# The front of an attention-plus-GLU kernel: value weights in two loads, a shorter inverse root, and another order of transpositions and products

## The chip, the cores and the metric

The kernel runs on one core of one Trainium2 chip. Its metric is the device time of one execution in microseconds; lower is better. Three runs of the kernel before gave 728.47, 729.49 and 730.18 us, so the median is 729.49 us.

## The reference

`x` is one sequence of 2048 tokens with 448 features. The output is `x` plus an attention branch plus a gated feed-forward branch, both fed by the same layer norm without scale and bias:

```
xn = (x - mean(x)) / sqrt(var(x) + 1e-5)
q, k, v = xn @ wq, xn @ wk, xn @ wv      # 16 heads of 28, four segments of 512 tokens
per segment: o = g * memory(q) + (1 - g) * softmax(q k^T / sqrt(28) + mask) v
             memory is then updated with phi(k)^T v and sum of phi(k)
h = sigmoid(xn @ w_gate) * (xn @ w_up)   # 448 -> 1792
out = x + o @ wo + h @ w_down
```

All values are float32. What matters here is the very beginning: the layer norm of the first segment, its transposition, and the products with `wv` and then with `wk` and `wq`.

## The kernel before, in words

**Numbers in two parts.** TensorE works on float32 operands in a rounded form ("high"). For exactness each operand is kept as a high part and the rest that rounding cut off ("low"), and a product is a sum over pairs high x high, high x low, low x high. 448 features are three chunks of 128 and one of 64. The lower half of chunk 3 of the activations holds the low part of its upper half, so a full product over 448 features takes eleven matrix instructions. The list `TERMS` (line 48) gives their order: for each chunk the three pairs, then the last two for chunk 3.

**Tiles.** A segment (a block `b`, four of them) is four tiles of 128 tokens. `acc[b]` holds the loaded `x`; `xs[b]` holds the normalised and transposed activations, high parts at chunk indices 0 to 3, low parts at 4 to 6 and in the lower half of chunk 3; `wv` and `wqk[c]` hold the split weights, high at 0 to 3, low at 4 to 7.

**What one tile of block 0 goes through.** VectorE takes mean and variance (`statistics`, lines 252 to 254). ScalarE takes the square root (`root`, 259). VectorE makes the reciprocal and refines it with one Newton step (`rstd`, 265 to 269), then normalises (`normalise`, 274) and copies 64 columns once more behind the row (275). TensorE transposes four pieces of 128x128 into one PSUM bank `pt` (96). ScalarE copies the bank to the high part of `xs` (98), VectorE subtracts to get the low part (99 for three chunks, 100 for the lower half of chunk 3). TensorE then makes the tile's values with eleven products into the bank `pv` (`values`, 284), and ScalarE moves them to `vst` (286).

**Weights.** `wv` arrives in four quarters, one for each chunk, in turns with the four tiles of `x` (349 and 350). Each quarter is rounded on ScalarE (365) and the rest subtracted on GpSimd (366). The weights for keys and queries arrive as seven chunks and are split the same way (370 and 371).

**What sets the order.** Within the front the queues of TensorE, ScalarE and VectorE hold the instructions in the order in which the program text issues them (`manual_schedule`, line 236), and each engine works through them in that order. So the text of lines 374 to 399, and the loop behind it, is the order table. It begins with `WARM` = 12 products of the identity with itself into a bank that nobody reads (375 and 376). After the fourth tile's values come seven groups of eleven products for keys and queries (`keys_queries`, 295, bank `pp`), during which VectorE and ScalarE also prepare block 1. Everything after that (feed-forward, attention, output) is one long list in which TensorE is nearly always busy.

Of the kernel before, what the change touches and what calls it, by code (L numbers as in the profile page):

```python
# [46 lines left out]

TERMS = [t for c in range(3) for t in ((c, c), (c, 4 + c), (4 + c, c))] + [(3, 3), (3, 7)]
# [4 lines left out]
WARM = 12  # L53
# [3 lines left out]
def kernel(  # L57
# [30 lines left out]
    def transpose_split(pt, src, dst, t):  # L88

        tok = slice(t * P, (t + 1) * P)  # L90
        for c in range(4):
            part = slice(c * P, (c + 1) * P)
            if src.dtype == F32R:
                T.transpose(pt[:, part].bitcast(F32R), src[:, part], ident_r)
            else:
                T.transpose(pt[:, part], src[:, part], ident)
        p3 = pt.rearrange("p (c n) -> p c n", c=4)
        A.activation(dst[:, 0:4, tok], p3, AF.Copy)  # L98
        V.tensor_sub(dst[:, 4:7, tok], p3[:, 0:3], dst[:, 0:3, tok].bitcast(F32))
        V.tensor_sub(dst[64:, 3, tok], p3[64:, 3], dst[64:, 3, tok].bitcast(F32))  # L100

# [134 lines left out]
    with tc.tile_pool(name="front", bufs=2) as sb, tc.manual_schedule(engines=FRONT):  # L236
# [9 lines left out]
        def statistics(b, t0, steps):  # L246
# [3 lines left out]
            ve = sb.tile([P, steps], F32, name=f"ve{steps}")  # L250
# [3 lines left out]
            V.tensor_scalar_add(ve, mv[:, :, 1], EPS)  # L254
            return mv, ve

        def root(ve):
            y = sb.tile([P, ve.shape[1]], F32, name=f"y{ve.shape[1]}")
            A.activation(y, ve, AF.Sqrt)
            return y  # L260

        def rstd(mv, ve, y):
            steps = ve.shape[1]
            tm = sb.tile([P, steps], F32, name=f"tm{steps}")
            V.reciprocal(y, y)
            V.tensor_mul(tm, y, y)
            V.tensor_mul(tm, tm, ve)
            V.tensor_scalar(tm, tm, -0.5, 1.5, op0=ALU.mult, op1=ALU.add)
            V.tensor_mul(y, y, tm)
            return [(mv[:, t, 0:1], y[:, t:t + 1]) for t in range(steps)]  # L270

        def normalise(b, t, mean, y):
            xn = sb.tile([P, 512], F32, name="xn")
            V.tensor_scalar(xn[:, :D], acc[b][:, t, :], mean, y, op0=ALU.subtract, op1=ALU.mult)
            (V if b == 0 else G).tensor_copy(xn[:, D:], xn[:, 384:D])
# [5 lines left out]
        def values(b, t):  # L281
            pv = bank("pv", "p")
            for n, (a, w) in enumerate(TERMS):
                T.matmul(pv[:, :D], xs[b][:, a, t * P:(t + 1) * P], wv[:, w, :],  # L284
                         start=n == 0, stop=n == len(TERMS) - 1)
            A.activation(vst[:, t, :, :DH], pv[:, :D].rearrange("p (h d) -> p h d", d=DH), AF.Copy)
# [59 lines left out]
        raw = [raw[t // 2][:, t % 2, :D] for t in range(4)]  # L346
        wv3 = w_v.rearrange("p (c n) -> p c n", c=4)
# [29 lines left out]
        mv, ve = statistics(0, 0, 1)  # L377
        y = root(ve)
        split_v(0)
        x0 = normalise(0, 0, *rstd(mv, ve, y)[0])  # L380
        split_v(1)
        split_v(2)
        mv, ve = statistics(0, 1, 1)
        y = root(ve)
        turn(0, 0, x0)
        split_v(3)
        x1 = normalise(0, 1, *rstd(mv, ve, y)[0])
        mv, ve = statistics(0, 2, 2)
        values(0, 0)
        turn(0, 1, x1)  # L390
        y = root(ve)
        st = rstd(mv, ve, y)
        split_qk(0)
        x2 = normalise(0, 2, *st[0])
        x3 = normalise(0, 3, *st[1])
        values(0, 1)
        turn(0, 2, x2)
        turn(0, 3, x3)
        split_qk(1)
        G.memset(heads, 1.0)  # L400
# [7 lines left out]
        for b in range(NB):  # L408
# [5 lines left out]
            for t in range(2 if b == 0 else 0, NT):  # L414
# [7 lines left out]
                if t == (3 if b == 0 else 0):  # L422
                    mv, ve = statistics(b + 1, 0, NT)
                if t == (3 if b == 0 else 0):
                    st = mv, ve, root(ve)
# [302 lines left out]
```

## Time and profile before

| what | value |
|---|---|
| median of three runs (lowest, highest) | 729.49 us (728.47, 730.18) |
| the profiled execution's own time | 728.81 us |
| span in the profile of that execution | 727.1 us |
| TensorE busy with matrix instructions | 708.5 us, 97% of the span |
| VectorE, ScalarE, GpSimd busy | 77%, 47%, 20% |
| first product for keys and queries starts | 26.04 us |
| first value product of block 1 starts | 51.25 us |

Times in the profile count from the start of the span, in microseconds. PE is TensorE, DVE is VectorE, ACT is ScalarE, POOL is GpSimd, SP issues the transfers. In a row of the timeline the first number is the start and the second the length; the name left of the arrow is written, the names right of it are read, xN is how many instructions the row joins, and the bracket gives the idle time ahead of it with what ended it. In a row of the table by windows each engine has its busy time and its count; then come the granted clock of TensorE (1.00 is full), the share of the transfer engines and the rate.

### The profile page before, as it was taken

To read this page: it belongs to the slowest core of one execution; us is meant where nothing else is said; L and a number is where in the kernel's file an instruction comes from. 1 tells how busy PE (TensorE), PEld (TensorE's weight loads), DVE (VectorE), ACT (ScalarE), POOL (GpSimd) and SP (SyncE) were. 2 spreads that over 40 slices of the span, in tenths; PEclk is the share of its full clock that TensorE was granted. 3 is DMA by queue.
4 is the path that set the end of the run, shared out by engine and by line. 5 is a ranking of instruction groups with operands and counts; after the bars stand their busy time and mean duration, and the time that the engine had idled before them with its cause. 6 is when DMAs were issued, how large, how long until landed. Compare 5 with 4: busy or idle time off the path is not lost.

```text
span 727.1 us, 10861 instructions
## 1 busy us (share of the span) xinstructions
PE 708.5 (97%) x3788; PEld 587.2 (81%) x3788; DVE 560.9 (77%) x1030; ACT 338.2 (47%) x552; POOL 147.9 (20%) x349
## 2 busy tenths in 40 slices
PE   7999999999999999999999999999999999998898
PEld 6888888887887877878878777787787877876697
DVE  5676776455599888898888898898788898888653
ACT  3635444231355554565545555455454555444320
POOL 4310000000131212222223223242222332322100
PEclk7999999999999999999999999999999999999999
DMA  9443546675343223322333225232422233223242
GB/s 311 185 174 133 218 178 236 227 252 134 98 106 86 74 66 94 107 78 67 109 103 88 59 83 133 71 88 79 127 66 73 64 92 85 82 74 110 84 159 89
DMA packets 58278, 86.24 MB, mean 119 GB/s; under 512 B 20080, under 2 KB 36976, under 8 KB 57712
## 3 DMA queue, kind: packets, MB, share of 16 engines
q1 hardware_dynamic: 56944, 81.88, 36.2%
q0 software_dynamic: 1280, 3.67, 1.4%
q8 instruction: 30, 0.49, 0.3%
q14 instruction: 24, 0.20, 0.1%
HBM read 53.81 MB, written 31.72 MB: 118 GB/s over the span
## 4 chain that ended last, share of the span: by engine, by line
PE 62%; DVE 18%; issue 8%; POOL 6%; ACT 3%; DMA 3%; SPq 0%; POOLq 0%; ACTq 0%; DVEq 0%
PE pgu L209 22%; PE pd L154 10%; PE pp L295 8%; PE pv L284 6%; PE po L668 5%; DVE mx L521 4%; DVE w L557 4%; PE st L506 3%; PE pa L583 3%; POOL w L518 2%; DVE acc L157 2%; DVE mb L549 2%; PE n L341 1%; PE pmm L323 1%; POOL on L595 1%
## 5 line engine op out<-in xcount | busy, mean ns | idle before, releaser
L209 PE MATMUL pgu<-xs,wgu 128*128 128x512 f32 x1232 | 321.7, 398 | 0.0
L209 PEld LDWEIGHTS pgu<-xs,wgu 128*128 128x128 f32 x1232 | 225.7, 188 | 44.9 <-issue 1.8
L154 PE MATMUL pd<-wdn,hh 128*128 128x448 f32 x672 | 165.3, 373 | 7.2 <-DVE acc L157 3.6
L154 PEld LDWEIGHTS pd<-wdn,hh 128*128 128x128 f32 x672 | 123.3, 190 | 23.7 <-DVE acc L157 3.7
L518 POOL TENSOR_SCALAR_AFFINE_SELECT w<-w 128x256 f32<-128x256 f32 (+1 forms) x160 | 72.1, 451 | 332.8 <-ACT w L509 330.9
L558 ACT ACTIVATE w<-w 128x1024 f32<-128x1024 f32 (+1 forms) x96 | 86.8, 914 | 84.3 <-DVE w L557 81.6
L521 DVE TRANSPOSE_TENSOR_REDUCE mx<-w 128x32 f32<-128x1024 f32 (+1 forms) x96 | 101.1, 1056 | 23.3 <-POOL w L518 23.1
L509 ACT ACTIVATE w<-st 128x512 f32<-128x512 f32 x160 | 93.5, 588 | 53.0 <-PE st L506 52.9
L557 DVE TENSOR_TENSOR w<-w,mb 128x1024 f32<-128x1024 f32 (+3 forms) x128 | 108.6, 872 | 0.4
L295 PE MATMUL pp<-xs,wqk 128*128 128x512 f32 x308 | 77.3, 399 | 0.0
L157 DVE TENSOR_TENSOR acc<-pd,acc 128x448 f32<-128x448 f32 x112 | 67.7, 606 | 8.0 <-PE pd L154 7.9
L295 PEld LDWEIGHTS pp<-xs,wqk 128*128 128x128 f32 x308 | 56.6, 189 | 11.8
L506 PE MATMUL st<-qk 84*128 84x128 f32 (+3 forms) x256 | 63.9, 311 | 0.0
L506 PEld LDWEIGHTS st<-qk 84*128 84x128 f32 x256 | 48.3, 189 | 8.9 <-ACT w L509 0.4
L220 ACT ACTIVATE hh<-sg 128x512 fp32r<-128x512 f32 x56 | 35.1, 626 | 43.5 <-DVE sg L218 38.4
L549 DVE STREAM_TRANSPOSE mb<-top 128x1024 f32<-128x1024 f32 x32 | 39.7, 1241 | 13.0 <-POOL top L546 12.9
L217 ACT ACTIVATE sg<-pgu 128x512 f32<-128x512 f32 x56 | 33.3, 595 | 34.7 <-PE pgu L209 34.5
L284 PE MATMUL pv<-wv,xs 128*128 128x448 f32 x176 | 42.2, 396 | 3.2 <-ACT xs L98 3.2
L221 DVE SCALAR_TENSOR_TENSOR hh<-sg,hh 128x512 fp32r<-128x512 f32 x56 | 39.6, 706 | 6.5 <-ACT hh L220 6.3
L218 DVE SCALAR_TENSOR_TENSOR sg<-sg,pgu 128x512 f32<-128x512 f32 x56 | 37.4, 668 | 9.0 <-PE pgu L209 8.8
L301 DVE TENSOR_TENSOR qk<-pp,qk 128x512 fp32r<-128x512 f32 x28 | 19.3, 690 | 30.7 <-ACT e L300 23.6
L284 PEld LDWEIGHTS pv<-wv,xs 128*128 128x128 f32 x176 | 35.0, 205 | 7.4 <-ACT xs L98 4.1
(94 smaller groups left out, 626.3 us busy)
## 6 DMA issues: line engine op xcount, KB each, us to landing
qk<-qd SPq DMA_DIRECT2D x192, 112.0 KB
qd<-qk SPq DMA_DIRECT2D x28, 512.0 KB
raw<-in_w_ffn SPq DMA_DIRECT2D x14, 512.0 KB
vd<-vst SPq DMA_DIRECT2D x4, 1024.0 KB
vv<-vd SPq DMA_DIRECT2D x16, 256.0 KB
od<-on POOLq DMA_DIRECT2D x16, 224.0 KB, 3.7
ob<-od SPq DMA_DIRECT2D x4, 896.0 KB
out<-acc SPq DMA_DIRECT2D x16, 224.0 KB
```

Of the source, the lines that this page charges most:

```text
L154: T.matmul(pd[:, :D], l, r, start=n == 0, stop=n == len(mms) - 1)
L157: V.tensor_add(acc[b][:, t, :], pd[:, :D], acc[b][:, t, :])
L209: T.matmul(dst, wgu[f][:, w, side * P:(side + 1) * P], xs[b][:, a, :], start=n == 0, stop=n == len(TERMS) - 1)
L284: T.matmul(pv[:, :D], xs[b][:, a, t * P:(t + 1) * P], wv[:, w, :], start=n == 0, stop=n == len(TERMS) - 1)
L295: T.matmul(pp, wqk[c][:, w, :], xs[b][:, a, :], start=n == 0, stop=n == len(TERMS) - 1)
L506: T.matmul(st[:, at:at + L - kb * P], self.qk[:KS, 1, h, kb * P:(kb + 1) * P], self.qk[:KS, 0, h, kb * P:], start=True, stop=True)
L509: A.activation(w, st, AF.Copy)
L518: G.affine_select(d, d, pattern=pattern, base=0, channel_multiplier=-1, compare_op=ALU.is_ge, fill=MASK)
L521: V.tensor_reduce(mx[:, 16 * n0:16 * (n + 1)], self.w[:, n0 * L:(n + 1) * L].rearrange("p (b n) -> p b n", n=32), axis=mybir.AxisListType. ...
L549: V.transpose(mb.rearrange("p h (b n) -> p (h b) n", n=32), top.rearrange("p h b -> p (h b)").unsqueeze(2).to_broadcast([P, 32, 32]))
L557: V.tensor_sub(w[:, :, a:b], w[:, :, a:b], mb[:, :, q0:])
L558: A.activation(w, w, AF.Exp, scale=SCALE)
```

## The change

Four things change, all in the front; the computation stays the same.

1. **Loads.** `wv` comes in two loads of two quarters each instead of four. The order on the queue is tile 0 of `x`, the first two quarters, tile 1, the last two quarters, then tiles 2 and 3 in one load.
2. **Inverse root.** The variance is kept as -0.5 (var + eps). For a single tile the Newton step is two instructions with per-partition scalars instead of four; for four tiles it is three instead of four. Tiles 2 and 3 of block 0 now have a chain each, where they shared one. The copy of 64 columns of block 0 moves from VectorE to ScalarE.
3. **Order.** Transpositions get ahead of products: tile 1 is turned ahead of the values of tile 0, tile 2 after seven of the eleven products of tile 1, tile 3 after seven of those of tile 2. Block 0 uses a list `EARLY` that takes high x high for all chunks first, then low activations, then low weights. The third chunk of the key weights is split one step earlier.
4. **Identity products.** 11 instead of 12 at the start, and 5 more between the transpositions of tile 0 and of tile 1.

```diff
+EARLY = [(c, c) for c in range(4)] + [(4 + c, c) for c in range(3)] + [(c, 4 + c) for c in range(4)]
-WARM = 12
+WARM = 11
...
-    def transpose_split(pt, src, dst, t):
+    def transpose_high(pt, src, dst, t):
...
         A.activation(dst[:, 0:4, tok], p3, AF.Copy)
+        return p3
+
+    def transpose_low(p3, dst, t):
+        tok = slice(t * P, (t + 1) * P)
         V.tensor_sub(dst[:, 4:7, tok], p3[:, 0:3], dst[:, 0:3, tok].bitcast(F32))
         V.tensor_sub(dst[64:, 3, tok], p3[64:, 3], dst[64:, 3, tok].bitcast(F32))
...
-            V.tensor_scalar_add(ve, mv[:, :, 1], EPS)
+            V.tensor_scalar(vh, mv[:, :, 1], EPS, -0.5, op0=ALU.add, op1=ALU.mult)
...
-            A.activation(y, ve, AF.Sqrt)
+            A.activation(y, vh, AF.Sqrt, scale=-2.0)
...
             V.reciprocal(y, y)
-            V.tensor_mul(tm, y, y)
-            V.tensor_mul(tm, tm, ve)
-            V.tensor_scalar(tm, tm, -0.5, 1.5, op0=ALU.mult, op1=ALU.add)
-            V.tensor_mul(y, y, tm)
+            if steps == 1:
+                V.tensor_scalar(tm, y, y, vh, op0=ALU.mult, op1=ALU.mult)
+                V.tensor_scalar(y, tm, 1.5, y, op0=ALU.add, op1=ALU.mult)
+            else:
+                V.tensor_mul(tm, y, y)
+                V.tensor_mul(tm, tm, vh)
+                V.scalar_tensor_tensor(y, tm, 1.5, y, op0=ALU.add, op1=ALU.mult)
...
-            (V if b == 0 else G).tensor_copy(xn[:, D:], xn[:, 384:D])
+            if b == 0:
+                A.activation(xn[:, D:], xn[:, 384:D], AF.Copy)
+            else:
+                G.tensor_copy(xn[:, D:], xn[:, 384:D])
...
-        for t in range(NT):
-            nc.sync.dma_start(acc[0][:, t, :], x[t * P:(t + 1) * P, :])
-            nc.sync.dma_start(raw[t], wv3[:, t, :])
+        nc.sync.dma_start(acc[0][:, 0, :], x[0:P, :])
+        nc.sync.dma_start(raw[0], w_v[:, :2 * D])
+        nc.sync.dma_start(acc[0][:, 1, :], x[P:2 * P, :])
+        nc.sync.dma_start(raw[1], w_v[:, 2 * D:])
+        nc.sync.dma_start(acc[0][:, 2:4, :], x[2 * P:L, :].rearrange("(t p) d -> p t d", p=P))
...
+        st[0] = statistics(0, 0, 1)
+        y[0] = root(st[0][1])
+        normalised(0)
         split_v(0)
+        st[1] = statistics(0, 1, 1)
         split_v(1)
+        y[1] = root(st[1][1])
+        turn_high(0)
+        fill(5)
+        normalised(1)
         split_v(2)
         split_v(3)
+        turn_low(0)
+        turn_high(1)
+        st[2] = statistics(0, 2, 1)
+        turn_low(1)
+        y[2] = root(st[2][1])
         values(0, 0)
+        normalised(2)
+        st[3] = statistics(0, 3, 1)
+        values(0, 1, lambda: turn_high(2))
+        turn_low(2)
+        y[3] = root(st[3][1])
         split_qk(0)
+        normalised(3)
+        values(0, 2, lambda: turn_high(3))
+        turn_low(3)
         split_qk(1)
+        split_qk(2)
```

How TensorE's queue begins, before (the number behind a name tells buffers apart; `pt` is a transposition, `pv` the values of a tile, `warm` the identity products):

```order
L376 MATMUL warm_151<-ident_60 128x128 x12
L96 MATMUL pt_195<-ident_60,xn_180 128x128 x4
L284 MATMUL pv_222<-wv_111,xs0_67 128x448 x11
L96 MATMUL pt_235<-ident_60,xn_211 128x128 x4
L284 MATMUL pv_259<-wv_111,xs0_67 128x448 x11
L96 MATMUL pt_272<-ident_60,xn_253 128x128 x4
L96 MATMUL pt_280<-ident_60,xn_256 128x128 x4
L284 MATMUL pv_293<-wv_111,xs0_67 128x448 x11
```

The same place of TensorE's queue in the changed kernel:

```order
L395 MATMUL warm_148<-ident_60 128x128 x11
L97 MATMUL pt_187<-ident_60,xn_172 128x128 x4
L398 MATMUL warm_148<-ident_60 128x128 x5
L97 MATMUL pt_211<-ident_60,xn_202 128x128 x4
L299 MATMUL pv_227<-wv_111,xs0_67 128x448 x11
L299 MATMUL pv_253<-wv_111,xs0_67 128x448 x7
L97 MATMUL pt_261<-ident_60,xn_244 128x128 x4
L299 MATMUL pv_253<-wv_111,xs0_67 128x448 x4
L299 MATMUL pv_285<-wv_111,xs0_67 128x448 x7
L97 MATMUL pt_293<-ident_60,xn_282 128x128 x4
```

The first value products moved behind the transposition of tile 1, and the transpositions of tiles 2 and 3 moved into the products of the tile ahead of them.

VectorE from the statistics of tile 1 to its normalisation, before (`ve` is the variance plus epsilon, `y` the root, `tm` a helper of the Newton step; line 99 and 100 are the low part of tile 0):

```order
L252 BN_STATS stats1_187<-acc0_71 128x6
L253 BN_AGGR mv1_188<-stats1_187 128x2
L254 TENSOR_SCALAR ve1_189<-mv1_188 128x1
L99 TENSOR_TENSOR xs0_67<-pt_195,xs0_67 128x3x128
L100 TENSOR_TENSOR xs0_67<-pt_195,xs0_67 64x128
L265 RECIPROCAL y1_193<-y1_193 128x1
L266 TENSOR_TENSOR tm1_205<-y1_193 128x1
L267 TENSOR_TENSOR tm1_205<-tm1_205,ve1_189 128x1
L268 TENSOR_SCALAR tm1_205<-tm1_205 128x1
L269 TENSOR_TENSOR y1_193<-y1_193,tm1_205 128x1
L274 TENSOR_SCALAR xn_211<-acc0_71,mv1_188,y1_193 128x448
L275 COPY xn_211<-xn_211 128x64
```

The same stretch of VectorE's queue in the changed kernel:

```order
L260 BN_STATS stats1_177<-acc0_71 128x6
L261 BN_AGGR mv1_178<-stats1_177 128x2
L262 TENSOR_SCALAR vh1_179<-mv1_178 128x1
L274 RECIPROCAL y1_185<-y1_185 128x1
L276 TENSOR_SCALAR tm1_198<-y1_185,vh1_179 128x1
L277 TENSOR_SCALAR y1_185<-tm1_198,y1_185 128x1
L286 TENSOR_SCALAR xn_202<-acc0_71,mv1_178,y1_185 128x448
L104 TENSOR_TENSOR xs0_67<-pt_187,xs0_67 128x3x128
L105 TENSOR_TENSOR xs0_67<-pt_187,xs0_67 64x128
```

The low part of tile 0 moved behind the normalisation of tile 1, two instructions of the root are gone, and the copy has left the engine.

ScalarE up to the high part of tile 1, in the changed kernel (line 384 rounds a quarter of `wv`, line 288 is the copy of 64 columns, line 99 the high part of a tile):

```order
L267 ACTIVATE y1_166<-vh1_162 128x1
L288 ACTIVATE xn_172<-xn_172 128x64
L384 ACTIVATE wv_111<-wv_raw_129 128x448 x2
L267 ACTIVATE y1_185<-vh1_179 128x1
L99 ACTIVATE xs0_67<-pt_187 128x4x128
L288 ACTIVATE xn_202<-xn_202 128x64
L384 ACTIVATE wv_111<-wv_raw_130 128x448 x2
L99 ACTIVATE xs0_67<-pt_211 128x4x128
```

Before, three quarters of `wv` stood between the root of tile 0 and the root of tile 1, and the fourth behind the high part of tile 0; now two stand there, and the last two follow the copy of tile 1.

More of the change, by code (lines that the diff above doesn't have):

```diff
@@ L413 @@
             st = None
-            for t in range(2 if b == 0 else 0, NT):
+            for t in range(3 if b == 0 else 0, NT):
                 values(b, t)
@@ L422 @@
                 if t == (3 if b == 0 else 0):
[L423 removed]
+                    mv, vh = statistics(b + 1, 0, NT)
                 if t == (3 if b == 0 else 0):
[L425 removed]
+                    st = mv, vh, root(vh)
                 if t == (3 if b == 0 else 2):
```

50 lines of the change are left out of this document (24 added, 26 removed).

## The prediction

> **What bounds the kernel now.** I first read the table by windows, cut at the first product for keys and queries and at the first value product of block 1.
>
> ```profile
> core 0: us, PE busy (x) PEld busy (x) DVE busy (x) ACT busy (x) POOL busy (x), PEclk, DMA share, GB/s
> 0.00:26.04 26.04, 20.82 (x85) 18.03 (x86) 16.89 (x51) 9.34 (x19) 9.65 (x17) 0.80 0.81 285
> 26.04:51.28 25.24, 25.06 (x143) 21.11 (x141) 18.54 (x39) 13.76 (x27) 6.49 (x9) 1.00 0.41 167
> 51.28:727.10 675.82, 662.62 (x3565) 548.02 (x3563) 525.45 (x942) 315.09 (x506) 131.77 (x324) 1.00 0.36 110
> ```
>
> After 26.04 PE is busy for 25.06 of 25.24 us and then 98% of the rest. So what the change is worth is how much earlier PE reaches 26.04, less what the later stages give back. Ahead of 26.04 PE idles for 5.2 us, and its clock is only 0.80 on average. Next, PE's own timeline:
>
> ```profile
> 1.54 5.03 PE L376 MATMUL warm<-ident 128*128 128x128 f32 x24 [1.54 <-POOL ident masks.py:199]
> 7.04 0.66 PE L96 MATMUL pt<-ident,xn 128*128 128x128 f32 x4 [0.47 <-DVE xn L274]
> 9.97 4.47 PE L284 MATMUL pv<-wv,xs 128*128 128x448 f32 x11 [2.28 <-ACT xs L98]
> 14.24 1.06 PE L96 MATMUL pt<-ident,xn 128*128 128x128 f32 x4
> 15.99 4.15 PE L284 MATMUL pv<-wv,xs 128*128 128x448 f32 x11 [0.69 <-ACT xs L98]
> 19.98 1.04 PE L96 MATMUL pt<-ident,xn 128*128 128x128 f32 x8
> 21.26 4.94 PE L284 MATMUL pv<-wv,xs 128*128 128x448 f32 x22 [0.25 <-ACT xs L98]
> 26.04 4.34 PE L295 MATMUL pp<-xs,wqk 128*128 128x512 f32 x18
> ```
>
> Tiles 0 and 1 take 4.27 and 3.99 us for eleven products, 0.37 each; tiles 2 and 3 take 26.04 - 21.26 = 4.78 for 22, so **0.217 each**. The clock explains it. It changes at 9.36 and 19.60, so I cut windows of 3.41 us from there; the clock is the third number from a row's end:
>
> ```profile
> 5.95:9.36 3.41, 1.28 (x10) 0.85 (x8) 2.06 (x6) 1.17 (x4) 1.50 (x2) 1.00 0.98 334
> 9.36:12.77 3.41, 2.79 (x8) 2.48 (x9) 2.58 (x8) 1.14 (x3) 2.33 (x3) 0.50 1.05 405
> 12.77:16.19 3.42, 2.73 (x10) 2.07 (x9) 2.12 (x8) 1.39 (x4) 0.00 (x0) 0.50 1.05 398
> 16.19:19.60 3.41, 3.41 (x10) 2.98 (x11) 3.14 (x10) 0.36 (x1) 1.28 (x1) 0.50 1.05 388
> 19.60:23.01 3.41, 3.16 (x19) 2.46 (x18) 1.99 (x6) 2.04 (x4) 0.72 (x1) 1.00 0.91 350
> 678.37:681.79 3.42, 1.92 (x12) 1.76 (x13) 1.79 (x5) 0.19 (x2) 0.00 (x0) 1.00 0.35 107
> 681.79:685.20 3.41, 3.41 (x38) 1.73 (x37) 1.08 (x3) 0.75 (x2) 0.00 (x0) 1.00 0.00 0
> ```
>
> PE busy for 1.28 of 3.41 us (38%) is followed by clock 0.50; 1.92 (56%) is followed by 1.00. At half clock 2.79 and 2.73 (82% and 80%) don't bring it back, a full window does. So PE goes slowly from 9.36 to 19.60 because it idled ahead of 9.36.
>
> **The change, part by part.**
>
> *When tile 1 is ready.* PE's first value product now stands behind the transposition of tile 1, so this chain sets its start. Its rows before, on DVE, ACT and POOL:
>
> ```profile
> 3.46 0.63 DVE L252 BATCH_NORM_STATS2 stats<-acc 128x6 f32<-128x448 f32 x1 [3.46 <-DMA acc<-in_x]
> 7.12 0.62 DVE L252 BATCH_NORM_STATS2 stats<-acc 128x6 f32<-128x448 f32 x1
> 7.99 0.15 DVE L254 TENSOR_SCALAR ve<-mv 128x1 f32<-128x1 f32 x1
> 10.87 0.16 DVE L265 RECIPROCAL y<-y 128x1 f32<-128x1 f32 x1
> 11.06 0.71 DVE L266 TENSOR_TENSOR tm<-y 128x1 f32<-128x1 f32 x1
> 12.00 0.15 DVE L268 TENSOR_SCALAR tm<-tm 128x1 f32<-128x1 f32 x1
> 12.38 0.51 DVE L274 TENSOR_SCALAR xn<-acc,mv,y 128x448 f32<-128x448 f32 x1
> 35.83 0.42 DVE L304 TENSOR_SCALAR e<-e 128x512 f32<-128x512 f32 x1
> ```
>
> ```profile
> 7.67 0.58 ACT L365 ACTIVATE wv<-wv_raw 128x448 fp32r<-128x448 f32 x1 [2.48 <-DMA wv_raw<-in_w_v]
> 8.77 0.58 ACT L365 ACTIVATE wv<-wv_raw 128x448 fp32r<-128x448 f32 x1 [0.52 <-DMA wv_raw<-in_w_v]
> 9.25 0.19 ACT L259 ACTIVATE y<-ve 128x1 f32<-128x1 f32 x1
> 9.34 0.58 ACT L98 ACTIVATE xs<-pt 128x512 fp32r<-128x512 f32 x1
> 9.96 0.58 ACT L365 ACTIVATE wv<-wv_raw 128x448 fp32r<-128x448 f32 x1
> 8.33 3.43 POOL L366 TENSOR_TENSOR wv<-wv_raw,wv 128x448 fp32r<-128x448 f32 x3 [1.91 <-ACT wv L365]
> ```
>
> Tile 1 of `x` is now the fourth block of 224 KB on the queue (tile 0 and two quarters go ahead). Before, the fourth block released ACT at 7.67, so I take **7.67**. If the bigger loads keep the 334 GB/s of the window from 5.95, three blocks behind the 3.46 at which tile 0 let DVE start take 2.1 us, 5.6; the upper end is the sixth block, 8.77. Statistics take 1.03 us from first start to last end (7.12 to 8.14): 8.70. The square root 0.19 with a hand-over of 0.04 makes 8.93. The new Newton step has two instructions with per-partition scalars, which nothing in the trace shows on one column. Below stands the 0.15 of L268; above 0.28, since L274 with such scalars takes 0.09 us more than L304 on 64 columns fewer. I take 0.20, nearer to the row of the same shape. Reciprocal, both and gaps of 0.03 make 0.7: 9.63; normalising 0.51: 10.14. L266 took 0.71 instead of 0.16 until POOL's row ended at 11.76, so a POOL row can hold DVE. POOL's first two pieces would end near 9.1 (half of the weights after 6 us, two pieces at 0.58 on ACT, two at 1.14 on POOL), so I count nothing here; cover gone, it is up to 0.5. The transposition's four pieces take 0.44 (the eight from 19.98 take 1.04 with the last one's tail, 0.11 a step), with the copy on ACT beside them. So the values begin at **10.75**, which is 0.8 later than before.
>
> *What PE then works through.* At full clock 44 products at 0.217 are 9.55, the transpositions of tiles 2 and 3 0.87. Before, tile 1 alone cost 14.24 to 15.99 between products; that is gone. Three waits remain.
> - The last quarters of `wv`: ACT has its copy for tile 1 ahead of them (10.4), then 0.58 twice, 11.4; POOL's fourth piece ends near 13.25. PE stands at its eleventh product at 10.75 + 2.17 = 12.9: **0.35**. All four high quarters, which `EARLY` needs first, are there when PE gets to them.
> - The low part of chunk 3, now the fourth product's operand: after the high part DVE needs 0.56 + 0.29:
>
> ```profile
> 9.95 0.56 DVE L99 TENSOR_TENSOR xs<-pt,xs 128x384 fp32r<-128x384 f32 x1 [1.81 <-ACT xs L98]
> 10.54 0.29 DVE L100 TENSOR_TENSOR xs<-pt,xs 64x128 fp32r<-64x128 f32 x1
> 16.62 1.28 POOL L371 TENSOR_TENSOR wqk<-stage,wqk 128x512 fp32r<-128x512 f32 x1 [4.87 <-ACT wqk L370]
> ```
>
>   The high part is there about when PE starts the tile, three products cover 0.65 of the 0.85, for two tiles: **0.4**, some of which the 0.217 already holds.
> - The turn of tile 3 in the middle of tile 2: DVE reaches its normalisation at about 17.65, just when POOL begins the 1.28 us of the first key chunk. PE asks for it at about 18. If POOL is first PE waits 1.1, if DVE is first 0.2. I take POOL first, **1.0**.
>
> Sum: 10.75 + 9.55 + 0.87 + 0.35 + 0.4 + 1.0 = 22.9, against 26.04: **3.1 us earlier**.
>
> *Does the clock stay?* Eleven identity products at half clock end near 6.3. Tile 0's root is shorter, and no POOL row lies beside it any more:
>
> ```profile
> 5.54 0.90 DVE L269 TENSOR_TENSOR y<-y,tm 128x1 f32<-128x1 f32 x1
> ```
>
> So tile 0 is turned from 6.3 to 6.75, and five products at 0.22 (0.42 of the first row, halved by the clock) run to 7.95. PE is then busy for about 2.0 to 2.1 of 3.41 us (60%), just above the 56% that kept the clock. From 10.2 on it is busy for 75% of the next window. So I take 1.00.
>
> *What is late next.* In the key stage PE hardly idles, but ACT and DVE are as late as PE there:
>
> ```profile
> 27.39 1.28 ACT L427 ACT_TABLE_LOAD   x1
> 30.51 1.54 DVE L304 TENSOR_SCALAR e<-e 128x512 f32<-128x512 f32 x1
> 37.03 0.66 PE L315 MATMUL pk<-ident,e 128*128 128x128 f32 x4 [0.18 <-DVE e L305]
> ```
>
> ACT's table load sits behind block 1's statistics (four tiles at 0.62 + 0.15 or so, 3 us, after tile 3's low part, which ends about 21; so about 24), and POOL splits three key chunks in a row at that time. If that holds the statistics' last step up, ACT is late by up to 1.2 us, which PE would pay at the row of 37.03. I count 0.3 and keep 0 and 1.2 as ends. Fewer transfers are issued, none of them waited for later; tile 2 and 3 land by 9.96 and are needed past 11.
>
> Net **2.8 us**. On the profiled execution's own 728.81 that gives 726.0. Its time lies 0.68 below the median; carried to the median of 729.49 the forecast is **726.7**. The ends of the unknowns (the load, of which at most 0.8 can be won before POOL's pieces hold DVE, to 1.1 lost; the scalars 0.15 each way; POOL not first, 0.8 won; the key stage 0.3 won to 0.9 lost), not all at one end together, make 725.0 to 728.0 for this case alone.
>
> **The rivals.**
> *The half clock was this execution's own.* The two changes lie 10.24 = 3 x 3.41 us apart, so the decision falls on a grid. With the grid elsewhere the 38% could be split between windows and the slow stretch be absent. Then before, tile 1 is ready when DVE is (13.1 + 0.44 + 0.65), the pieces behind it move up by about 1.65, and PE reaches the key stage at 24.4. The change gains only 24.4 - 22.9 - 0.3 = 1.2 to 1.4: **728.1**. For it: nothing ties the grid to the kernel's start. Against: the profiled time with the slow stretch is not above the timed runs. The Trainium skill (TensorE: Matmul & The Clock Gate, Part 1: The HAM clock gate) says that the window is free-running and doesn't restart with the kernel; by that rule such executions exist. The same section names an idle window as what lowers the clock; here a window 38% busy lowered it, and the measurement decides.
>
> *The clock falls all the same.* If 60% isn't enough, PE runs at half clock from 10.75 to 16.19 and loses 2.7 less the waits that this hides, 2.3. The gain is 0.5: **729.0**.
>
> *The key stage takes it back.* ACT late by 1.2 and more: gain 1.7, **727.8**.
>
> *Slower.* Tile 1 waits behind half of `wv`, and PE has put all value products behind it. Each microsecond that tile 1 lands later PE starts later, and past about 8.9 the window from 9.36 is too empty to hold the clock. With tile 1 at 9.96, the last landing before, PE starts at 13.05, is slow to 19.60 (17 products), then 27 at 0.217, 0.87 and 1.3 of waits: 27.7, which is 1.7 late: **731.2**. For it: the early windows moved bytes slowest. Against: the fourth block was there at 7.67.
>
> **How the numbers follow.** Forecast 0.50, own clock grid 0.20, clock falls 0.13, key stage 0.10, slower 0.07. A measurement of this kernel can tell about 0.2%, 1.46 us: faster means below 728.03, slower above 730.95. Faster: 0.50, half of the grid's 0.20 and over half of the key stage's 0.10, 0.65. Slower 0.06. The rest, 0.29, is within. The range 725.0 to 729.4 leaves out the slower case and part of the falling clock.
>
> **What would show it.** Right: the key stage starts at 22 to 24, the clock reads 1.00 in the windows from 9.36, PE's first value product starts at 10.3 to 11.2, the eleven products of each of tiles 0 and 1 take about 2.5 us each. Wrong: clock 0.50 there; a wait of `x` for tile 1 past 8; an idle row of PE ahead of `pk` in the key stage above 0.5.

## The result and the profile after

The changed kernel took **728.55 us** (median of 20 runs, 726.59 to 732.64) beside 728.76 us for the kernel before (20 runs). The ratio is 1.0004 with an interval of 0.9991 to 1.0016, so no difference can be told. (It isn't the quotient of the two medians, which would be 0.9997.) The forecast was 726.7 us. The range of 725.0 to 729.4 holds the result, but the forecast case, 2.8 us faster, did not come. The profiled execution was one of the shortest: 726.59 us, span 724.9.

The table by windows of after, cut at the same two places as before (the last numbers of a row are clock, transfer share and rate):

```profile
core 0: us, PE busy (x) PEld busy (x) DVE busy (x) ACT busy (x) POOL busy (x), PEclk, DMA share, GB/s
0.00:22.26 22.26, 18.89 (x92) 15.84 (x93) 15.01 (x42) 10.41 (x24) 8.74 (x17) 1.00 0.91 330
22.26:47.53 25.27, 25.04 (x142) 21.08 (x141) 19.25 (x41) 13.86 (x27) 7.26 (x9) 1.00 0.42 171
47.53:724.89 677.36, 662.51 (x3566) 547.89 (x3564) 525.53 (x940) 314.80 (x506) 129.72 (x324) 1.00 0.36 110
```

The key stage starts at 22.26 instead of 26.04, and block 1's values at 47.53 instead of 51.28. So 3.7 to 3.8 us are won there. But the third stage lasts 677.36 us instead of 675.82: 1.5 us of the gain are lost behind the front, even in this short execution. PE's timeline of the front:

```profile
1.54 5.07 PE L395 MATMUL warm<-ident 128*128 128x128 f32 x22 [1.54 <-POOL ident masks.py:199]
6.40 1.06 PE L97 MATMUL pt<-ident,xn 128*128 128x128 f32 x4
7.25 1.33 PE L398 MATMUL warm<-ident 128*128 128x128 f32 x10
9.19 0.66 PE L97 MATMUL pt<-ident,xn 128*128 128x128 f32 x4 [0.61 <-DVE xn L286]
9.61 2.51 PE L299 MATMUL pv<-wv,xs 128*128 128x448 f32 x10
12.28 1.89 PE L299 MATMUL pv<-wv,xs 128*128 128x448 f32 x8 [0.17 <-POOL wv L385]
14.01 0.60 PE L97 MATMUL pt<-ident,xn 128*128 128x128 f32 x4
14.37 2.91 PE L299 MATMUL pv<-wv,xs 128*128 128x448 f32 x11
18.27 0.68 PE L97 MATMUL pt<-ident,xn 128*128 128x128 f32 x4 [1.00 <-DVE xn L286]
18.70 3.72 PE L299 MATMUL pv<-wv,xs 128*128 128x448 f32 x15
22.26 7.82 PE L312 MATMUL pp<-xs,wqk 128*128 128x512 f32 x33
```

The order of the change is plain to see: tile 1 is turned ahead of all values, tiles 2 and 3 within the products of the tile ahead. Ten products take 2.51 us, where eleven took 4.47, because the clock reads 1.00 throughout. DVE's rows for tiles 1 and 3, and POOL's beside them:

```profile
5.84 0.63 DVE L260 BATCH_NORM_STATS2 stats<-acc 128x6 f32<-128x448 f32 x1
7.38 0.27 DVE L276 TENSOR_SCALAR tm<-y,vh 128x1 f32<-128x1 f32 x1
7.68 0.21 DVE L277 TENSOR_SCALAR y<-tm,y 128x1 f32<-128x1 f32 x1
7.93 1.20 DVE L286 TENSOR_SCALAR xn<-acc,mv,y 128x448 f32<-128x448 f32 x1
16.93 1.28 DVE L286 TENSOR_SCALAR xn<-acc,mv,y 128x448 f32<-128x448 f32 x1
```

```profile
6.67 2.22 POOL L385 TENSOR_TENSOR wv<-wv_raw,wv 128x448 fp32r<-128x448 f32 x2 [4.29 <-ACT wv L384]
16.69 1.28 POOL L390 TENSOR_TENSOR wqk<-stage,wqk 128x512 fp32r<-128x512 f32 x1 [4.46 <-ACT wqk L389]
```

Tile 1 is worked on at 5.84 with no wait ahead, so its load was there. Both normalisations take 1.2 us and more instead of 0.51, each ending just behind the POOL row that began before it.

**Where the gain goes.** Going through PE's rows of both profiles side by side, after is 3.8 us ahead from the key stage on, and still 3.9 ahead at 164 us. Near 436 us the lead shrinks. There PE waits for ACT's copy of `pa`, which stands in ACT's queue behind the split of a feed-forward weight load. ACT's two rows and PE's row of before:

```profile
437.78 1.06 ACT L82 ACTIVATE wgu<-raw 128x1024 fp32r<-128x1024 f32 x1 [0.49 <-DMA raw<-in_w_ffn]
438.75 0.58 ACT L586 ACTIVATE w<-pa 128x512 f32<-128x512 f32 x1
```

```profile
439.38 0.66 PE L590 MATMUL n<-ident,w 128*128 128x128 f32 x4 [0.88 <-ACT w L586]
```

The same rows of after:

```profile
434.72 1.06 ACT L83 ACTIVATE wgu<-raw 128x1024 fp32r<-128x1024 f32 x1 [1.29 <-PE pd L162]
435.69 0.58 ACT L625 ACTIVATE w<-pa 128x512 f32<-128x512 f32 x1
```

```profile
436.32 0.66 PE L629 MATMUL n<-ident,w 128*128 128x128 f32 x4 [1.69 <-ACT w L625]
```

The wait ahead of `n` is 1.69 us instead of 0.88. That is 0.8 of the 1.5 us. The lead is then 3.1 us, still 3.0 at 640 us and 2.4 at the end; b_again, the kernel before once more, loses 0.9 between 640 and 676 us against the same profile, so nothing ties that last 0.6 to the change. The change touches none of the lines near 436 us. (The bracket of ACT's split names PE's `pd`, which ended at 434.63 here; the last part of the load, the split's other wait, came at 434.64.) What this load has to do with the front is what most of the experiments are about.

### The profile page after: what moved, and what is told of

Read it like the earlier page. It is cut to its first block, busy times and chain, and to the rows that moved or that the text cites. A ratio compares the mean times of both kernels' runs of the same rounds, so it can differ in the third digit from the quotient of the medians.

```text
span 724.9 us, 10868 instructions
## 1 busy us (share of the span) xinstructions
PE 706.4 (97%) x3796; PEld 584.8 (81%) x3796; DVE 559.8 (77%) x1021; ACT 339.1 (47%) x557; POOL 145.7 (20%) x349
## 4 chain that ended last, share of the span: by engine, by line
PE 65%; DVE 18%; issue 7%; POOL 5%; ACT 3%; DMA 2%; POOLq 0%; SPq 0%; ACTq 0%
PE pgu L217 25%; PE pd L162 11%; PE pp L312 8%; PE po L707 5%; PE pv L299 4%; DVE mx L560 4%; DVE w L596 3%; PE st L545 3%; PE pa L622 3%; DVE acc L165 2%; DVE mb L588 2%; POOL w L557 2%; PE n L358 2%; PE pmm L340 1%; POOL on L634 1%
## 5 line engine op out<-in xcount | busy, mean ns | idle before, releaser
L313 ACT ACTIVATE qk<-pp 128x512 fp32r<-128x512 f32 x28 | 16.7, 597 | 50.5 <-PE pp L312 34.4
L707 PE MATMUL po<-wo,xs 128*128 128x448 f32 x176 | 39.2, 372 | 1.1 <-DVE acc L165 1.1
```

Of the source, the lines that this page charges most:

```text
L707: T.matmul(po[:, :D], xs[b][:, a, t * P:(t + 1) * P], wo[w // 4][:, D * (w % 4):D * (w % 4 + 1)], start=m == 0, stop=m == len(TERMS) - 1)
```

## The experiments

Each kernel ran beside runs of the kernel before on the same chip. This table has what the profiles show of each. "Slow windows" are stretches of 3.41 us with clock 0.50 ahead of the key stage. The last three columns concern the place near 436 us: SP's time from the issue of the weight load to the next issue, ACT's from that issue to the split, and PE's wait ahead of `n`. The times are in us. The last five kernels exchange two of ACT's instructions at this place, which is explained below.

| kernel | loads in the front | ratio to before (95%) | key stage starts | slow windows | load to next issue | issue to split | wait |
|---|---|---|---|---|---|---|---|
| before | 8 | | 26.04 | 3 | 0.77 | 3.93 | 0.88 |
| b_again | 8 | 1.0003 (0.9993 to 1.0012) | 24.41 | 1 | 0.77 | 4.05 | 1.00 |
| b_fill | 8 | 0.9994 (0.9984 to 1.0004) | 23.99 | 0 | 0.77 | 4.17 | 1.12 |
| a_8loads | 8 | 0.9981 (0.9969 to 0.9993) | 22.77 | 0 | 0.77 | 4.00 | 0.95 |
| after | 5 | 1.0004 (0.9991 to 1.0016) | 22.26 | 0 | 0.46 | 4.72 | 1.69 |
| a_again | 5 | 1.0003 (0.9993 to 1.0013) | 22.51 | 0 | 0.46 | 5.84 | 2.80 |
| a_nofill | 5 | 1.0008 (0.9997 to 1.0018) | 23.62 | 1 | 0.46 | 6.02 | 2.98 |
| b_5loads | 5 | 1.0021 (1.0009 to 1.0032) | 24.59 | 1 | 0.47 | 5.11 | 2.07 |
| a_8more | 5 + 8 | 0.9989 (0.9974 to 1.0004) | 22.64 | 0 | 0.45 | 4.67 | 1.61 |
| b_swap | 8 | 0.9980 (0.9971 to 0.9988) | 23.83 | 0 | | | none |
| b_swap_again | 8 | 0.9978 (0.9967 to 0.9989) | 23.41 | 0 | | | none |
| a_swap | 5 | 0.9969 (0.9957 to 0.9980) | 22.53 | 0 | | | none |
| a_swap_again | 5 | 0.9959 (0.9944 to 0.9974) | 22.48 | 0 | | | none |
| a_swap_late | 5 | 0.9961 (0.9948 to 0.9975) | 21.87 | 0 | | | none |

### Both kernels again

Neither was changed. The question was whether the first two profiles stand for the kernels.

> The changed kernel unchanged, profiled once more and timed. The two profiles on hand differ by 3.77 us at the first key product and by 2.2 us at the end, the timed medians by 0.2 us. Theory A (half clock elsewhere): in most executions of the changed kernel more windows of 3.41 us run at clock 0.50 than the one in the profile (granted clock 0.990 to 0.995 instead of 0.997), and they lie in the last 70 us; the key stage still starts at 22 to 23 and the time stays at 728 to 729. Theory B (the front's own grid): the extra slow windows lie ahead of 26 us, and the key stage starts at 24 or later.

> The kernel before unchanged, profiled once more and timed. Theory A: the slow stretch from 9.4 to 19.6 us is there again or at least in most executions, key stage at 25.5 to 26.2, granted clock about 0.990. Theory B: in another execution the slow stretch is shorter or absent, key stage at 24 to 24.7, granted clock 0.993 or more, so that the profile on hand showed the front of before slower than it usually is. Time 728.5 to 729 by both.

Both ratios are 1.0003. The front of after is nearly the same again (22.51), that of before is not: 24.41 instead of 26.04, with one slow window instead of three. And a_again loses more than after near 436 us. PE's rows there, of after and of a_again:

```profile
436.73 2.79 PE L217 MATMUL pgu<-xs,wgu 128*128 128x512 f32 x11
```

```profile
437.81 0.66 PE L629 MATMUL n<-ident,w 128*128 128x128 f32 x4 [2.80 <-ACT w L625]
438.23 4.36 PE L217 MATMUL pgu<-xs,wgu 128*128 128x512 f32 x11
```

The wait is 2.80 us, and the same eleven products behind it take 4.36 us instead of 2.79: the window of 3.41 us that holds the wait was followed by half clock, which cost another 1.6 us. The window and the next one:

```profile
435.61:439.02 3.41, 1.21 (x8) 1.07 (x9) 1.71 (x3) 1.54 (x2) 0.01 (x1) 1.00 0.73 144
439.02:442.43 3.41, 3.41 (x10) 2.64 (x9) 3.41 (x7) 0.00 (x0) 0.00 (x0) 0.50 0.02 5
```

PE is busy for 1.21 us (35%) there. In a_nofill a wait of 2.98 us lies across two windows with 2.19 and 1.66 us of work (64% and 49%), and the clock stayed. The lead of a_again over before, 3.5 us at the key stage, is 0.4 at 442 us and gone at 445. So both theories have a part in it: some of the front's gain depends on the execution of before that it is compared with, and what is left is given back later, but at 436 us and not only in the last 70 us.

The extra slow windows of theory A are there as well. a_again has one at 681.36 us that after hasn't, and it costs 1.5 us. Eight of the fourteen profiles of this study fall to half clock twice in the tail, the second time near 680 us; three of them have before's order of the front and five that of after. So the spans of two single profiles can differ by 1.5 us for that alone. Theory C in the texts below is that this place gives the gain back, and that the three fewer issues on SP are why; its rival D is chance.

### Identity products added, and taken away

b_fill puts them into before, behind the turn of tile 0:

```diff
         turn(0, 0, x0)
+        for _ in range(5):
+            T.matmul(warm[:, :P], ident, ident, start=True, stop=True)
         split_v(3)
```

> The kernel before with five identity products between the transpositions of tile 0 and its values, and nothing else. They lie in a wait of 2.27 us. If the front's half clock costs time in most executions (theory A), the clock holds past 9.4, the key stage starts near 24.4 and the time falls by about 1.5 us to 727.2. If the half clock was one execution's own (theory B), the time stays within 0.4 us of before.

a_nofill takes them out of after:

```diff
-WARM = 11
+WARM = 12
         turn_high(0)
-        fill(5)
         normalised(1)
```

> The changed kernel without its five identity products in the wait (and 12 at the start as before). Theory A: PE idles from 7 to 9 us, the clock may fall at the next decision, key stage 1 to 2.5 us later than in the changed kernel. Theory B: since tile 1 follows tile 0 by 2 us only, the wait is too short to lower the clock in most executions; key stage within 0.5 us of the changed kernel, time within 0.5 us.

The windows of a_nofill, b_swap and b_fill in which PE waits for the first tiles, each with the one that follows:

```profile
7.15:10.57 3.42, 1.51 (x11) 1.08 (x9) 2.93 (x10) 1.84 (x6) 2.18 (x3) 1.00 1.02 377
10.57:13.98 3.41, 3.41 (x10) 2.91 (x10) 3.16 (x10) 0.79 (x3) 1.96 (x2) 0.50 1.05 405
```

```profile
7.67:11.08 3.41, 1.86 (x10) 1.26 (x9) 1.88 (x7) 1.77 (x5) 3.24 (x3) 1.00 1.03 366
11.08:14.49 3.41, 2.47 (x12) 1.43 (x10) 3.10 (x12) 1.28 (x4) 0.17 (x1) 1.00 1.05 407
```

```profile
6.59:10.01 3.42, 2.46 (x19) 1.98 (x17) 1.84 (x6) 2.14 (x5) 2.04 (x2) 1.00 0.98 333
10.01:13.42 3.41, 2.94 (x15) 2.03 (x13) 3.10 (x11) 0.83 (x3) 1.35 (x2) 1.00 1.05 405
```

Without the five products PE is busy for 1.51 of 3.42 us (44%), the clock falls, and the key stage starts 1.1 to 1.4 us later than in the profiles of after. With them in before it is busy for 2.46 (72%) and the clock stays. But in b_swap, whose front is that of before, the window begins 1.72 us later than before's 5.95, PE is busy for 1.86 of 3.41 (55%), and the clock stays as well. So the products do what they are for, and whether they are needed depends on where the windows lie in that execution. In the ratios neither kernel differs from its model by more than the intervals. For b_fill the interval also leaves out the 1.5 us that theory A promised.

The share of a window doesn't settle the matter by itself. b_again has 1.77 us of work (52%) in two windows of its front. The clock stayed at 1.00 behind the first and fell to 0.50 behind the second:

```profile
5.00:8.41 3.41, 1.77 (x14) 1.34 (x13) 2.93 (x9) 1.23 (x3) 1.98 (x2) 1.00 0.99 321
11.83:15.24 3.41, 1.77 (x9) 1.09 (x9) 3.18 (x10) 1.86 (x4) 0.20 (x1) 1.00 1.05 402
```

### The copy ahead of the split

One line in each kernel lets ACT issue its copy of `pa` ahead of the split of the eleventh weight load (weights `f` = 10); `copies` collects these copies in the order of the text:

```diff
-            split_weights(wgu[f], raw_up[f].rearrange("p (c n) -> p c n", c=4))
+            with tc.issue_after(copies[-2].ins) if f == 10 else nullcontext():
+                split_weights(wgu[f], raw_up[f].rearrange("p (c n) -> p c n", c=4))
...
-            A.activation(at, pa, AF.Copy)
+            copies.append(A.activation(at, pa, AF.Copy))
```

> The kernel after, but ACT's copy of pa near 436 us (w<-pa, on which PE's transposition n waits) is issued ahead of the split of the eleventh feed-forward weight load (wgu<-raw), which waits for its DMA; in before and after it stands behind it. Nothing is left out. Both theories on why that load is late agree here: PE's wait ahead of n falls from 1.69 us (after) to 0.6 or 0.7, the 0.58 us of the copy with its hand-over. Theory C (the gain of the front is given back at this place): the key stage still starts at 22 to 24 us, and the median is 1.0 to 2.0 us below after's, at about 727.5. Rival (the gain is lost in the tail whatever comes before): the median stays within 0.5 us of after's.

> The kernel before with the same exchange on ACT near 438 us. Nothing is left out. There the wait is 0.88 us, so at most 0.2 to 0.3 us can be won: the median within 0.5 us of before's by theory C. Rival (the exchange is worth something by itself, through ACT's or DVE's order behind it): over 0.8 us faster than before, as in the kernel after with the exchange.

ACT and PE in a_swap:

```profile
433.60 0.60 ACT L626 ACTIVATE w<-pa 128x512 f32<-128x512 f32 x1
434.95 1.06 ACT L83 ACTIVATE wgu<-raw 128x1024 fp32r<-128x1024 f32 x1 [0.75 <-DMA raw<-in_w_ffn]
```

```profile
434.72 0.60 PE L630 MATMUL n<-ident,w 128*128 128x128 f32 x4
```

The wait ahead of `n` is not 0.6 but gone, as PE has `pd` products to do meanwhile. The split still waits for its load, and nobody waits for the split. a_swap is 2.3 us faster than before (0.0031 of 728.56) and so 2.5 us faster than after (1.0004), more than the 1.0 to 2.0 of theory C. b_swap is 1.5 us faster than before. That is what I had written down for the rival, that the exchange is worth something by itself; theory C gave 0.2 to 0.3, since I had counted on 0.6 of the wait to stay. So the exchange helps both kernels, and after by about 1 us more. The same two kernels for a sharper size:

> The kernel a_swap, unchanged: after with ACT's copy of pa ahead of the split of the eleventh weight load. With b_swap_again it shows what the change is worth where nothing is given back near 436 us. Theory C: 0.9968 of before within 0.001. By the key stage's starts in profiles whose clock stays at 1.00 in the front (22.5 against 23.8 to 24.0) a_swap is 1.3 us below b_swap, more where the front's clock falls in b_swap. Rival (the change is worth nothing even then): the two within 0.3 us.

> The kernel b_swap, unchanged: before with ACT's copy of pa ahead of the split of the eleventh weight load. Theory C: 0.9985 of before, since the wait of 0.88 us is gone (a reading of 0.998 as in the first run would say that a fallen clock behind that wait is saved too in some executions). Rival: 0.997, the same as a_swap_again.

a_swap_again is within theory C's 0.001. b_swap_again is not at its 0.9985 but at 0.9978, where its text has a clock that no longer falls behind the wait in some executions. The mean granted clock of the timed runs points that way: 0.9924 in before beside 0.9948 in b_swap, 0.9932 beside 0.9940 in the second pair, where one window at half clock is 0.0023 of an execution. Where those windows lie is not on record, so this is not shown.

With nothing to lose at 436 us, the change is worth 0.0011 in the first pair (0.9980 to 0.9969) and 0.0019 in the second, 0.8 and 1.4 us. That is about the 1.3 us between the key stages of a_swap and b_swap (22.53 and 23.83), and half or less of the 2.8 that I forecast. The intervals of the two kernels overlap in both pairs, so the size is not sharp.

### The loads alone, both ways

a_8loads keeps all of after but brings the same blocks in eight loads, in the same order:

```diff
-        nc.sync.dma_start(raw[0], w_v[:, :2 * D])
-        nc.sync.dma_start(acc[0][:, 1, :], x[P:2 * P, :])
-        nc.sync.dma_start(raw[1], w_v[:, 2 * D:])
...
+        for part in ("x0", "w0", "w1", "x1", "w2", "w3", "x2", "x3"):
+            t = int(part[1])
+            if part[0] == "x":
+                nc.sync.dma_start(acc[0][:, t, :], x[t * P:(t + 1) * P, :])
+            else:
+                nc.sync.dma_start(raw[t], wv3[:, t, :])
```

> The kernel after with value weights and x in eight loads again (in after's order of bytes: tile 0, two quarters, tile 1, two quarters, tiles 2 and 3), so SP issues as many DMAs as in before. Nothing is left out. Theory C (three fewer issues on SP move what goes by count on its queue, among it the fetch of instructions that comes 3.2 to 3.5 us after the issue of the eleventh weight load in after, 2.6 to 2.9 us in before): the split of that load comes 3.9 to 4.2 us after its issue again, PE's wait ahead of n is about 0.9 us, and the median is 1 to 1.5 us below after's. Rival D (chance of slow packets): the split comes 4.7 to 6.0 us after the issue, and the wait stays at 1.7 to 3.4. For the front: if two loads instead of four carry part of the gain, the first value product starts later than 9.61 us; by the prediction's price of an issue it moves by at most 0.3 us.

b_5loads puts after's five loads into before, and nothing else of the change:

```diff
-        for t in range(NT):
-            nc.sync.dma_start(acc[0][:, t, :], x[t * P:(t + 1) * P, :])
-            nc.sync.dma_start(raw[t], wv3[:, t, :])
+        nc.sync.dma_start(acc[0][:, 0, :], x[0:P, :])
+        nc.sync.dma_start(raw[0], w_v[:, :2 * D])
+        nc.sync.dma_start(acc[0][:, 1, :], x[P:2 * P, :])
+        nc.sync.dma_start(raw[1], w_v[:, 2 * D:])
+        nc.sync.dma_start(acc[0][:, 2:4, :], x[2 * P:L, :].rearrange("(t p) d -> p t d", p=P))
```

> The kernel before with after's five loads alone (tile 0, half of the value weights, tile 1, the other half, tiles 2 and 3); everything else as before. Nothing is left out. Theory C: three fewer issues on SP put the fetch 3.2 to 3.5 us after the eleventh weight load's issue, its split comes 4.7 to 6.0 us after the issue, PE's wait ahead of n grows from 0.9 to 1.7 or more, and the median is 0.8 to 2 us above before's, less what the front gains. Rival D: split after 3.9 to 4.1 us, wait 0.9. For the front: tile 1 can be worked on about 1.8 us earlier, but PE's order has tile 1 behind tile 0's products, so the key stage starts within 0.7 us of before's 24.0 to 26.0.

At this place both came as theory C had it. PE's row of a_8loads, then that of b_5loads:

```profile
436.25 0.66 PE L630 MATMUL n<-ident,w 128*128 128x128 f32 x4 [0.95 <-ACT w L626]
```

```profile
438.79 0.66 PE L592 MATMUL n<-ident,w 128*128 128x128 f32 x4 [2.07 <-ACT w L588]
```

With eight loads the wait is back at 0.95 and the kernel is 1.4 us faster than before; with five loads in the old front it is 2.07 and the kernel 1.5 us slower. In the table the four kernels with eight loads wait 0.88 to 1.12, those with five 1.61 to 2.98. Row by row beside before's profile, PE loses 0.7 to 3.5 us between 435 and 445 us in the five profiles with five loads, 1.7 in the mean, and 0.1 to 0.2 in b_again, b_fill and a_8loads. **So the loads cost about 1.5 us (0.7 to 2.3 by b_5loads' interval), and they cost it where nothing of the front runs any more.** The front itself hardly uses them: with eight, the first value product starts at 10.11 instead of 9.61 to 9.97 in the six profiles with five loads and the identity products. That is 0.1 to 0.5 later, where I had given at most 0.3.

### Eight more issues

The trace has a fetch of instructions (8 KB on the instruction queue) beside that load: 2.6 to 2.9 us after its issue with eight loads, 3.2 to 3.5 with five. This kernel moves the fetch away:

```diff
         nc.sync.dma_start(gate, beta.partition_broadcast(P))
+        spare = sb.tile([P, 8, 16], F32, name="spare", bufs=1)
+        for n in range(8):
+            nc.sync.dma_start(spare[:, n, :], x[0:P, 0:16])
```

> The kernel after (with its five loads) and eight more issues on SP behind the front's loads: each brings 128x16 numbers of x into a spare tile that nobody reads. Nothing is left out. The program's DMAs use eight semaphores in turn, so eight more issues leave every later DMA with the semaphore that it has in after; the fetch of SP's instructions, if it goes by count, comes eight issues earlier, ahead of the eleventh weight load. Theory C with the fetch as the cause: no fetch 2.6 to 3.6 us after that load's issue, its split 3.6 to 4.2 us after the issue, PE's wait ahead of n 0.65 to 0.95 us, the median about 1.5 us below after's. Rival (the semaphores' turn is the cause): the split 4.7 to 6.0 us after the issue, the wait 1.7 to 3.4 us, the median as after's.

The fetch moved to 420.5, and yet the split comes 4.67 us after the issue and PE waits 1.61. So it isn't the fetch that delays the load, and that half of theory C falls. Both numbers are those of the rival, to within 0.1 us. The time (0.9989) lies between the two cases and decides nothing. What does fit all kernels shows in SP's queue. Its rows of before, after and a_8more:

```profile
433.85 0.36 SPq L164 DMA_DIRECT2D raw<-in_w_ffn  x1
434.62 2.47 SPq L490 DMA_DIRECT2D qk<-qd  x6
```

```profile
430.00 0.36 SPq L172 DMA_DIRECT2D raw<-in_w_ffn  x1
430.46 2.73 SPq L529 DMA_DIRECT2D qk<-qd  x6
```

```profile
418.01 2.70 SPq L532 DMA_DIRECT2D qk<-qd  x6
430.37 0.36 SPq L172 DMA_DIRECT2D raw<-in_w_ffn  x1
430.82 2.52 SPq L532 DMA_DIRECT2D qk<-qd  x6
```

In before SP stands still for 0.41 us between the end of the weight load's issue and the six small loads of `qk` behind it; in after for 0.10. The missing 0.3 us is a pause of SP, which in after lies two issues further on (six issues take 2.73 instead of 2.47), and in a_8more in the six issues ahead of the weight load (2.70). It goes by SP's count of instructions: it comes three instructions later where the front has three issues fewer, and eight earlier where it has eight more. In all fourteen traces it stands ahead of SP's 336th instruction, and another like it ahead of the 208th, 128 earlier. The fetch follows 1.3 to 2.6 us behind. So in the kernels with eight loads the pause happens to give the weight load a head start of 0.77 us over the loads of `qk`; in all others it is 0.45 to 0.47, and the load's last parts may compete with theirs. The trace has its completion in sixteen parts: in before all by 3.85 us after the issue; in after thirteen by 3.29, the last at 4.65. With the kernels of the exchange counted in, the last part comes at 3.85 to 4.08 in the six profiles with the head start and at 4.36 to 5.94 in the eight without it. The rival (the eight semaphores in turn) fits as well: the load signals one and the same of them in all six, and another one in all eight. So that the loads of the front make this load late is shown, and that the head start is the way is argued; a kernel that delays the `qk` loads by other means wasn't tried.

### The key chunk behind the normalisation

In a_swap, with `split_qk(0)` behind tile 3's normalisation:

```diff
-        split_qk(0)
         normalised(3)
+        split_qk(0)
         values(0, 2, lambda: turn_high(3))
```

> The kernel a_swap with the split of the first key chunk (ACT's high part, POOL's low part) issued behind the normalisation of tile 3 instead of ahead of it. Nothing is left out. In after PE waits 1.00 us ahead of the turn of tile 3, because DVE's normalisation takes 1.28 us instead of 0.51 beside POOL's row of the first key chunk. If POOL's row is what holds DVE, the normalisation takes 0.5 to 0.6 us and starts when its root is ready, PE's wait falls to 0 to 0.3 us, and the key stage starts at 21.6 to 21.9 instead of 22.5: 0.7 to 0.9 us off the median of a_swap if nothing gives it back. Rival (DVE is late by its own chain): the normalisation gets shorter but the wait stays above 0.6. Second rival (the key chunks' low parts come late instead): an idle row of PE ahead of pp or pk above 0.3 us.

DVE's and PE's row for tile 3 in a_swap_late:

```profile
17.31 0.51 DVE L287 TENSOR_SCALAR xn<-acc,mv,y 128x448 f32<-128x448 f32 x1
```

```profile
17.88 0.68 PE L97 MATMUL pt<-ident,xn 128*128 128x128 f32 x4 [0.22 <-DVE xn L287]
```

The normalisation is back at 0.51, PE waits 0.22 instead of 1.00, and the key stage starts at 21.87, 0.6 earlier. No row of PE with a wait above 0.3 stands ahead of `pp` or `pk`. In the time nothing shows (0.9961 beside 0.9959 of a_swap_again), and intervals of 0.0014 either way can't tell 0.6 us. The fastest kernels of the study are a_swap, in two readings 0.9969 and 0.9959 of before, and a_swap_late, which can't be told from it.

## Why the prediction was right and wrong

**When tile 1 is ready: right in kind, three sizes off.** Tile 1 was there by 5.84, not 7.67, near the 5.6 that the prediction worked out from bytes and rate and kept as an end; in the other profiles with after's order and five loads its last part landed between 5.57 and 6.90. The two instructions with per-partition scalars took 0.27 and 0.21, within the bounds of 0.15 and 0.28 (0.20 taken). POOL's first pieces, for which I counted nothing, ran from 6.67 to 8.89 and made the normalisation 0.69 longer, above the 0.5 that I gave as its price. The first value product came at 9.61 instead of 10.75, outside the 10.3 to 11.2 that were to show it right. (The terms named add up to 10.14 + 0.44 = 10.58; the other 0.17 have no row.)

**What PE works through: right sum, one term small.** From the first value product to the key stage I had 9.55 + 0.87 + 0.35 + 0.4 + 1.0 = 12.2; it took 12.65. The wait for tile 3 is 1.00 as forecast, from the cause given: POOL first. The wait for `wv` is 0.17 (0.35), the transpositions 0.36 + 0.43 (0.87). The products with the gaps between them take the remaining 10.7 instead of 9.95. If those gaps are the waits for low parts, which no row shows by itself, the 0.4 should have been 1.1. The key stage began at 22.26 (22.9).

The Trainium skill (SBUF — State Buffer, SBUF: two separate sides) says that VectorE and GpSimd share a port pair as an exclusive lock, held for the whole instruction by whichever starts first, where the VectorE instruction works in a two-port mode or has two inputs in SBUF. The trace agrees as to who waits: POOL started at 16.69 and DVE at 16.93, and DVE's row took 1.28 us; without POOL beside it, in a_swap_late, 0.51. It ended 0.24 us behind POOL's, less than 0.51, so whether DVE stood still all that time is not shown.

**Does the clock stay? Right.** It reads 1.00 ahead of the key stage in all seven profiles with this front and the five products, and in a_nofill it falls for one window. In the seven, PE's emptiest window ahead of the key stage is 58% to 79% busy, where I had reckoned with 60%. The share alone doesn't settle it, as the two windows with 52% in b_again show.

**What is late next: not there.** The key stage lasted 25.27 us instead of 25.24; I had counted 0.3.

**The base of the sum: 1.9 us too late.** I set 22.9 against 26.04. In the four profiles that have before's front unchanged (before, b_again, b_swap, b_swap_again) the key stage starts at 26.04, 24.41, 23.83 and 23.41, the middle 24.1. After's front (after, a_again, a_swap, a_swap_again) has 22.26 to 22.53, the middle 22.5. So by these few profiles the front gains 1.6 us, and not 3.1 or 3.8. My rival of the execution's own grid had this at 0.20, with 24.4 for before; three of the four profiles are its case. How many of the timed executions are is not on record. The Trainium skill (TensorE: Matmul & The Clock Gate, Part 1: The HAM clock gate) says that the window runs freely and doesn't restart with the kernel. The trace agrees: the same front has three, one, none and none slow windows.

**"Fewer transfers are issued, none of them waited for later": the step that failed.** I looked only at who waits for the loads of the front. With three fewer issues a weight load came in later 400 us on, and ACT had a copy for PE queued behind that load's split. (The way there, a pause in SP's queue that no longer keeps six small loads off the large one, is argued.) b_5loads prices it at 1.5 us lost against before, a_8loads at 1.6 us won back against after (0.9981 beside 1.0003 and 1.0004).

**The sum as it was measured:** 1.6 us won in the front, 1.5 lost at 436 us, next to nothing left, as the 1.0004 says. That is neither my forecast nor one of my rivals: the nearest, 728.1, had the first half of the reason. That the range holds 728.55 is luck. Its upper end was meant for a falling clock, which did not come, and the kernel before turned out at 728.76 instead of the 729.49 from which the forecast counts, which brought the two 0.7 us nearer.

## What to carry to other kernels

A start-up gain that rests on one execution's clock should be read from several profiles before it is promised, since the clock's windows lie elsewhere each time. Where an engine's queue holds a copy that the bound engine needs soon behind an instruction that waits for a transfer, put the copy first: that was worth more here than the whole change, and it takes away the dependence on when the transfer lands. Count the issues of a queue as part of a change, because what follows by count moves with them, hundreds of microseconds later too.

## What was not expected of the hardware

- SP pauses for about 0.3 us at places fixed by its instruction count, ahead of the 208th and of the 336th in all fourteen traces, and behind the second an 8 KB fetch on the instruction queue follows 1.3 to 2.6 us later. Three issues fewer, or eight more, moved the pause by three and by eight instructions.
- A 512 KB load reports in sixteen parts. Where the first of six loads of `qk` was issued 0.46 instead of 0.77 us behind it, its last part came at 4.4 to 5.9 us instead of 3.9 to 4.1.
- Windows with PE busy for 35%, 38% and 44% were followed by half clock, windows with 55%, 56% and 72% by full clock, and 52% by either (b_again). At half clock 80% was followed by half clock in before and by full clock in a_nofill (2.73 us of work at 676.17). So no single share decides here, either way.
